# Copies and casts of a fused attention and gated-convolution kernel moved from ACT to DVE and POOL, with a new order table

## The chip, the core and the metric

The kernel runs on one core of one Trainium2 chip. The metric is the device time of one execution in microseconds (us), lower is better; three executions of the kernel before are given. Besides the times there is one profiled execution with its trace. The engines are PE (matmul; PEld is its weight load), DVE, ACT, POOL, and SP, which here only issues DMAs.

## What is computed

The reference, cut to what matters (B = 4, H = 8 heads, S = 768, D = 64, so d_model = 512):

```python
k_sum = k.reshape(B, H, 24, 32, D).max(axis=3)
v_sum = v.reshape(B, H, 24, 32, D).mean(axis=3)
scores = concat([where(|i - j| < 16, q @ k.T / 8, -1e9), q @ k_sum.T / 8 + log(32)])
a = softmax(scores)
x = (a @ concat([v, v_sum])).transpose(0, 2, 1, 3).reshape(B, S, 512)
gate = sigmoid(sum over 5 taps k of conv_w[k] * x shifted by 4 - k)
out = (gate * (x @ w_val)) @ w_out
```

## The kernel before, in words

The work is cut into 24 units u (batch, third of the sequence, half of the heads; six units to a batch) and 12 groups g = u // 2 of 256 rows. Each step of a unit or group is a small function `op_X`, and the table `ORDER` (L51) lists about 1,130 tokens such as `S.7.0` (step S of unit 7, part 0). The program is emitted token by token in this order, so the table sets the order of every engine's queue and of SP's DMA issues; an engine takes its own tokens in turn and waits at the first that isn't ready. All instructions of one engine stay in the table's order, whatever the others do.

The steps, with lines and engines as they are before:

- Loads by SP: `k` (484 KB), `q` (512 KB), `v` (512 KB), `n` (values, 256 or 384 KB), `w` and `o` (the two weight matrices, four parts each of 512 KB), `m`, `i`, `c`; `f` copies a block of rows of `v` in the buffer.
- `ks` (L307, L310, DVE) block maxima of k, `kc` (L315, POOL) copies them into the k tile. `S` (L438, PE, 16 matmuls) scores, `N` (L454, DVE, 4 instructions) mask and row minimum, `E` (L468, ACT, 4 instructions) exponential, `R` (DVE) reciprocal, `M` (L481, POOL) scaling.
- `T` (L490, PE, 16 transposes) into PSUM, `C` (L494, ACT) copies it out, `X` (L508, PE, 32 matmuls) attention times values.
- The result x of a unit is read out of PSUM by `F` (L519, ACT, as f32), `H` (L516, ACT, rounded), and `I` (L533, ACT, times the last tap, into the PSUM tile g, one of two halves). `A` (L538, DVE, eight per unit) adds the other taps, `G` (L544, ACT) is the tanh of the gate, `L` (L524, POOL) the rest of x after rounding.
- `V` (L558, PE) is x times w_val: 24 matmuls, 16 in group 0; `gf` (L563, DVE) gates it; `gh` (L567, ACT) rounds it and `gl` (L572, POOL) takes the rest; `O` (L587, PE, 12 matmuls, 8 in group 0) is the last product; `oe` (L597, ACT) brings it out of PSUM and `st` (L606, SP) stores it. `oe` writes a tile `ob` with two buffers, so the third needs the store of an earlier one to have landed.
- The weights are split on chip: `wvs`/`wos` (ACT), `wvd`, `wve`, `wod`, `woe` (DVE), then the rounded part `wvc`/`woc` (`high_part`, ACT or, with a trailing 1, POOL), then `wvb`/`wob` (POOL). `pw` are eight blocks of matmuls on a constant, early in the program.

PSUM is given out by `psum_plan` from the same table: scores S and transposes T share a ring of two pairs of banks, everything else a ring of four. A PE step whose place in the ring is still held by an earlier tile waits until that tile's last reader is through.

Of the kernel before, what the change touches and what calls it, by code (L numbers as in the profile page):

```python
# [56 lines left out]
wve.1 ce T.0 E.3.2 q.2 S.4.0 S.4.1 N.4.3 N.4.0 n.0.5 pw.5 E.1.1 E.1.3 E.1.0 VB.5 pw.7 VB.3 R.1 R.3
N.4.1 w.2 M.1.1 C.0.0 C.0.1 wvc.1 wvd.2 w.3 wvs.3 wvd.3 N.4.2 v.0.0 M.1.0 wvs.2 wve.2 wve.3 VB.1
vb.0 pw.2 wvb.1 h.0 S.5.0 S.5.1 N.5.2 N.5.0 wvc.3.1 M.3.1 M.3.0 N.5.3 v.0.1 N.5.1 vb.1 T.1 C.1.0
k.1.0 ks.1.0 wvb.3 wvc.2.1 C.1.1 X.0 I.0.0 F.0 I.0.1 A.0.0 A.0.1 X.1 F.1 I.1.0 A.1.0 T.2 n.1.3 v.1.1  # L60
o.0 E.5.0 v.1.0 tr.1.3.1 wvb.0 A.0.2 A.0.3 I.1.1 V.0.0 E.5.1 E.4.1 k.1.1 A.1.1 n.1.1 E.4.3 C.2.0
E.4.2 kc.1.0 A.0.4 A.1.2 A.0.5 A.1.3 A.0.6 E.5.3 A.1.4 A.0.7 G.0 A.1.5 C.2.1 q.3 ks.1.1 kc.1.1 wvb.2
# [636 lines left out]
```

## Time and profile before

| | us |
|---|---|
| three executions | 234.11, 232.50, 232.01 |
| median | 232.5 |
| profiled execution, its own time | 233.51 |
| its span in the trace (first to last instruction) | 231.4 |
| PE busy / DVE / ACT / POOL in the span | 218.8 / 171.0 / 187.1 / 150.9 |

The span is what the trace can explain; the remaining 2.1 us of the profiled execution lie around it. The granted PE clock is full speed in every slice. PE is busy 95% of the span, but a busy PE is not a PE at its best, since the time of a matmul in the trace includes waits inside a block; so the argument counts blocks of PE work by their price when they follow each other closely.

### The profile page before, as it was taken

Reading aid. Unit: us, or ns where it says so; the run is one execution under the profiler, and the core shown is the slowest. Engines: PE = TensorE matmul, PEld = TensorE weight load, DVE = VectorE, ACT = ScalarE, POOL = GpSimd, SP = SyncE. Lnnn points to the kernel's source line nnn. Section 1 sums busy time; section 2 is a strip of 40 time slices with the busy share of each in tenths; the row PEclk is TensorE's granted clock in tenths of the full one; section 3 lists DMA queues with packets and bytes.
Section 4 is the critical chain, followed back from the end, with each engine's and each line's share of the span. In section 5 each row is a group of like instructions: output and inputs, shape, how many; then the busy total and the mean of one; then the engine's idle time right before and its main releaser. Section 6 shows DMA issues by size and latency. Waiting matters only on the chain.

```text
span 231.4 us, 7645 instructions
## 1 busy us (share of the span) xinstructions
PE 218.8 (95%) x2828; PEld 185.3 (80%) x2828; DVE 171.0 (74%) x699; ACT 187.1 (81%) x614; POOL 150.9 (65%) x207
## 2 busy tenths in 40 slices
PE   2699999989999989999999999999999999999993
PEld 2475687638998867999789899988989898899882
DVE  1698989989999988869998859639729848555600
ACT  2399899999999979998999987798996698553320
POOL 2125897987999999956497869699069419044040
PEclk9999999999999999999999999999999999999999
DMA  6999999995986946828915634540449310102122
GB/s 235 341 389 369 408 410 281 406 364 179 318 353 217 283 174 219 305 82 290 284 29 184 183 118 140 180 177 3 130 145 319 89 48 19 46 0 93 45 91 91
DMA packets 17052, 46.50 MB, mean 201 GB/s; under 512 B 2136, under 2 KB 3160, under 8 KB 17016
## 3 DMA queue, kind: packets, MB, share of 16 engines
q1 hardware_dynamic: 17016, 46.02, 57.1%
q8 instruction: 22, 0.36, 0.6%
q14 instruction: 14, 0.11, 0.2%
HBM read 37.56 MB, written 6.29 MB: 190 GB/s over the span
## 4 chain that ended last, share of the span: by engine, by line
PE 66%; DMA 18%; ACT 10%; DVE 4%; issue 1%; SPq 1%; ACTq 0%
PE out L587 23%; PE val L558 23%; DMA k<-in_kT_dram 7%; PE s L438 7%; PE x L508 7%; DMA raw_wo<-in_wo_dram 5%; ACT p L468 4%; PE pt L490 4%; DMA out_dram<-ob 3%; DMA qbd<-in_qT_dram 3%; DVE g L538 2%; PE pw L332 1%; PE vb L342 1%; ACT g L533 1%; DVE sn L454 1%
## 5 line engine op out<-in xcount | busy, mean ns | idle before, releaser
L538 DVE SCALAR_TENSOR_TENSOR g<-xf,cwt,g 128x256 f32<-128x256 f32 x192 | 87.5, 484 | 14.3 <-ACT g L533 8.6
L468 ACT ACTIVATE p<-sn,nm 128x120 f32<-128x120 f32 x192 | 74.0, 396 | 10.5 <-DVE nm L454 10.3
L481 POOL TENSOR_TENSOR p<-p,ri 128x480 f32<-128x480 f32 x48 | 46.8, 991 | 23.9 <-DVE ri L476 21.5
L558 PE MATMUL val<-xh,wv 128*128 128x256 f32 x352 | 49.6, 283 | 0.0
L454 DVE CUSTOM_DVE_ANT_0 sn<-s,mask 128x120 f32<-128x120 f32 x192 | 42.7, 276 | 6.0 <-PE s L438 4.5
L558 PEld LDWEIGHTS val<-xh,wv 128*128 128x128 f32 x352 | 44.5, 188 | 1.4 <-issue 0.3
L587 PE MATMUL out<-wo,gh 128*128 128x512 f32 x176 | 45.1, 398 | 0.0
L572 POOL TENSOR_TENSOR gl<-gf,gh 128x512 fp32r<-128x512 f32 x22 | 28.3, 1294 | 18.1 <-ACT gh L567 18.0
L468 ACT ACTIVATION_READ_ACCUMULATOR p<-sn,nm 128x1 f32 x192 | 38.3, 200 | 0.0
L587 PEld LDWEIGHTS out<-wo,gh 128*128 128x128 f32 x176 | 31.7, 188 | 6.9 <-ACT gt L544 0.2
L524 POOL TENSOR_TENSOR xl<-xf,xh 128x512 fp32r<-128x512 f32 x22 | 28.2, 1292 | 7.9 <-ACT xh L516 7.8
L438 PE MATMUL s<-k,qbd 64*64 64x120 f32 x768 | 26.3, 280 | 6.9 <-POOL k L315 2.7
L438 PEld LDWEIGHTS s<-k,qbd 64*64 64x64 f32 x768 | 21.0, 139 | 11.1 <-POOL k L315 3.9
L326 POOL TENSOR_TENSOR vT<-vT 128x384 f32<-128x384 f32 (+3 forms) x48 | 27.3, 570 | 2.8
L597 ACT ACTIVATE ob<-out 128x512 f32<-128x512 f32 x23 | 13.7, 597 | 18.1 <-PE out L587 14.5
L558 PE MATMUL val<-xl,wv 128*128 128x256 f32 x176 | 27.7, 279 | 0.0
L494 ACT COPY pts<-pt 120x512 f32<-120x512 f32 x48 | 26.3, 589 | 1.5 <-PE pt L490 1.4
L508 PEld LDWEIGHTS x<-pts,v 120*64 120x64 f32 x768 | 23.6, 138 | 3.7 <-ACT pts L494 1.1
L508 PE MATMUL x<-pts,v 120*64 120x64 f32 x768 | 25.4, 224 | 0.4 <-DVE low_wo L394 0.4
L563 DVE SCALAR_TENSOR_TENSOR gf<-gt,val 128x512 f32<-128x512 f32 x24 | 16.4, 685 | 11.9 <-PE val L558 5.7
L587 PE MATMUL out<-wo,gl 128*128 128x512 f32 x88 | 24.1, 395 | 0.0
L558 PEld LDWEIGHTS val<-xl,wv 128*128 128x128 f32 x176 | 23.7, 188 | 0.0
(55 smaller groups left out, 259.1 us busy)
## 6 DMA issues: line engine op xcount, KB each, us to landing
v<-in_vw_dram SPq DMA_DIRECT2D x24, 512.0 KB
k<-in_kT_dram SPq DMA_DIRECT2D x16, 484.0 KB
out_dram<-ob SPq DMA_DIRECT2D x23, 256.0 KB
qbd<-in_qT_dram SPq DMA_DIRECT2D x11, 512.0 KB
vT<-in_vT_dram SPq DMA_DIRECT2D x12, 384.0 KB
raw_wv<-in_wv_dram SPq DMA_DIRECT2D x4, 512.0 KB
raw_wo<-in_wo_dram SPq DMA_DIRECT2D x4, 512.0 KB
v<-vs SPq DMA_DIRECT2D x18, 96.0 KB
```

The costliest lines, as they stand in the source:

```text
L326: nc.gpsimd.tensor_tensor(dst, src[:, :, :n], src[:, :, n : 2 * n], ALU.add)
L438: nc.tensor.matmul(sp[64 * e : 64 * e + 64, h, c * KW : c * KW + KW], qbd[g % NQB][64 * h : 64 * h + 64, pr, i * QT : i * QT + QT], ktile( ...
L454: nc.vector.tensor_tensor_reduce(sn[:, n, :], tiles["s", u][:, h, c * KW : c * KW + KW], mask[:, mv, :], -1.0 / math.sqrt(D), 3.0e38, ALU.add,
L468: nc.scalar.activation(p[:, n, :], tiles["sn", u][:, n, :], AF.Exp, bias=tiles["nm", u][:, n : n + 1], scale=-1.0, accum_out=rs[:, u % NRS ...
L481: nc.gpsimd.tensor_tensor(p[:, w], p[:, w], ri[:, w].unsqueeze(2).broadcast_to([P, TPU, KW]), ALU.mult)
L494: nc.scalar.copy(pts[:, :, QT * e : QT * e + QT], tiles["pt", u][:KW, e])
L508: nc.tensor.matmul(dst, w, src, start=True, stop=True)
L524: nc.gpsimd.tensor_tensor(xl[:, prs(u), :], xf(g)[:, prs(u), HALO:], tiles["xh", g][:, prs(u), :].bitcast(F32), ALU.subtract,)
L538: nc.vector.scalar_tensor_tensor(gt, xf(u // NHP)[:, pr, o : o + SG], cwt[:, pr, o : o + 1], gt, ALU.mult, ALU.add)
L558: nc.tensor.matmul(val[:, r], w, x, start=(n == 0), stop=(n == len(terms) - 1))
L572: nc.gpsimd.tensor_tensor(gl[:, cos, :], tiles["gf", g, cp], tiles["gh", g][:, cos, :].bitcast(F32), ALU.subtract)
L587: nc.tensor.matmul(po, x, w, start=(n == 0), stop=(n == len(terms) - 1))
```

## The change

Six steps get an optional last argument `alt`; a token that carries it as a trailing 1 runs on another engine:

- `C`, `H`, `F`, `I`, `oe` (copies out of PSUM): DVE rather than ACT, by a new helper `copy` (tensor_copy, or tensor_scalar with a factor).
- `gh` (cast of the gated values, SBUF to SBUF): POOL rather than ACT.
- `wvc`/`woc` could do so before; three more now do (all eight on POOL).

The same steps are all there: none is added or removed. Of the tokens that change engine, 11 are `C`, 11 `I`, 8 `H`, 3 `F`, 3 `oe` (36 copies to DVE), 15 `gh` and 3 weight casts (18 to POOL). `vb` gets the argument too, but no token uses it. The order table is new from the first token to the last, and with it the queues, the order of the loads and the places in PSUM. The diff, cut:

```diff
-    def op_C(u, e):
+    def copy(dst, src, scale=None, alt=0):
+        if alt and scale is None:
+            nc.vector.tensor_copy(dst, src)
+        elif alt:
+            nc.vector.tensor_scalar(dst, src, scale, None, ALU.mult)
+        elif scale is None:
+            nc.scalar.copy(dst, src)
+        else:
+            nc.scalar.activation(dst, src, AF.Copy, scale=scale)
+
+    def op_C(u, e, alt=0):
         pts = wt(("pts", u), [KW, NP, P], "pts")
-        nc.scalar.copy(pts[:, :, QT * e : QT * e + QT], tiles["pt", u][:KW, e])
+        copy(pts[:, :, QT * e : QT * e + QT], tiles["pt", u][:KW, e], alt=alt)
...
-        nc.scalar.activation(gt[:, r], src, AF.Copy, scale=cwt[:, pr, NK - 1 : NK])
+        copy(gt[:, r], src, cwt[:, pr, NK - 1 : NK], alt)
...
-        nc.scalar.copy(gh[:, 2 * cp : 2 * cp + 2, :], tiles["gf", g, cp])
+        (nc.gpsimd.tensor_copy if alt else nc.scalar.copy)(
+            gh[:, 2 * cp : 2 * cp + 2, :], tiles["gf", g, cp]
+        )
...
-            nc.scalar.activation(ob, po, AF.Copy, scale=0.5)
+            copy(ob, po, 0.5, alt)
```

Some lines of the new table that the text below speaks of: the loads and DVE work ahead of `S.7.0`, the stretch after it, and one of the late stores.

```diff
+woe.1 F.2 E.5.1 o.2 wos.2 v.2.1 H.2 E.5.3 L.3 L.2 h.2 wod.2 woe.2 O.0.1 O.0.0 N.6.2 E.6.2 N.6.3 R.5
+N.8.1 N.8.2 M.5.1 I.2.0 N.6.0 I.3.0 k.1.2 N.6.1 ks.1.2 oe.0.1 E.6.3 I.3.1 E.6.0 k.1.3 v.2.0 M.5.0
+ks.1.3 n.1.3 A.3.0 N.8.3 N.8.0 I.2.1 kc.1.2 woc.2.1 kc.1.3 T.4 A.2.0 A.3.1 E.6.1 R.6 st.0.1 tr.1.3.1
+A.2.1 A.3.2 S.7.0 E.8.1 C.4.0 f.2.0 C.4.1 oe.0.0 S.7.1 N.7.3 E.7.3 f.2.1 X.4 n.1.1 tr.1.1 woc.0.1
...
+E.17.2 C.14.0.1 oe.4.0 A.12.6 h.7 O.4.1 v.7.1 gf.6.1 C.15.1.1 R.17 f.7.1 k.3.1 ks.3.1 A.12.7 C.14.1
+kc.3.3 n.3.2 v.8.1 C.15.0 tr.3.1 X.15 I.15.1.1 st.4.0 E.16.2 oe.4.1 E.16.3 st.4.1 I.15.0 H.15.1 F.15
...
+X.16 H.16.1 I.16.0 X.17 v.9.1 st.3.1 F.16 F.17 I.16.1 S.20.1 S.21.0 S.20.0 h.9 gh.7.1.1 L.16 N.20.0
```

## Rows read from the trace of the kernel before

**Rows 1.** The page, part 1: busy time, share of the span, instructions
```profile
PE 218.8 (95%) x2828; PEld 185.3 (80%) x2828; DVE 171.0 (74%) x699; ACT 187.1 (81%) x614; POOL 150.9 (65%) x207
```

**Rows 2.** Stages: length, busy of PE, PEld, DVE, ACT, POOL; PEclk, DMA, GB/s
```profile
40.00:50.00 10.00, 9.72 (x126) 5.89 (x126) 8.88 (x36) 10.00 (x33) 9.42 (x14) 1.00 1.03 407
50.00:60.00 10.00, 9.37 (x174) 7.70 (x173) 9.89 (x51) 9.87 (x42) 8.28 (x13) 1.00 0.67 221
60.00:70.00 10.00, 10.00 (x122) 9.60 (x121) 9.72 (x44) 9.95 (x32) 9.43 (x12) 1.00 0.92 337
70.00:80.00 10.00, 10.00 (x144) 7.97 (x144) 9.42 (x36) 9.97 (x35) 9.65 (x15) 1.00 0.85 262
80.00:87.00 7.00, 5.73 (x92) 4.50 (x91) 6.17 (x14) 5.50 (x17) 6.69 (x13) 1.00 0.50 173
...
120.00:140.00 20.00, 20.00 (x273) 18.18 (x269) 15.75 (x73) 18.29 (x62) 15.23 (x23) 1.00 0.45 142
```

**Rows 3.** PE in order of time: start, us, line, operation, idle before and releaser
```profile
51.85 0.64 PE L438 MATMUL s<-k,qbd 64*64 64x120 f32 x16 [0.63 <-DVE nm L454]
...
87.05 1.46 PE L438 MATMUL s<-k,qbd 64*64 64x120 f32 x48 [1.32 <-ACT pts L494]
```

**Rows 4.** The chain that ended last: start, us until the next piece, what
```profile
39.64 8.94 DMA k<-in_kT_dram
...
49.62 0.79 DVE g L538 x2
...
52.00 0.65 DVE ks L307
52.65 0.26 DVE ks L310
...
57.71 2.27 ACT p L468 x12
...
63.44 1.04 ACT gh L567 x2
64.48 0.75 ACT g L533 x2
...
69.29 0.47 ACT pts L494
...
77.90 7.94 DMA out_dram<-ob
...
99.05 0.44 PE vsp L358 x4
...
102.12 1.80 PE s L438 x64
...
112.50 1.09 PE pt L490 x32
113.59 2.97 PE out L587 x12
...
118.36 2.02 PE x L508 x64
120.38 8.68 PE val L558 x72
...
213.90 13.87 PE out L587 x60
```

**Rows 5.** DVE in order of time, two 512-wide instructions back to back
```profile
43.94 0.68 DVE L563 SCALAR_TENSOR_TENSOR gf<-gt,val 128x512 f32<-128x512 f32 x1
44.54 0.68 DVE L402 SCALAR_TENSOR_TENSOR wf<-sc_wo,low_wo 128x512 uint32<-128x512 uint32 x1
```

**Rows 6.** Groups by line: busy us, mean ns of one; a cast on POOL
```profile
L409 POOL CAST wo<-wf 128x512 fp32r<-128x512 f32 x2 | 1.2, 612 | 0.1
```

**Rows 7.** The casts' partner gl (L572) on POOL in two stages: length, busy
```profile
60.00:80.00 20.00, 3.90 (x3) 1.00 0.88 299
200.00:231.40 31.40, 5.09 (x4) 1.00 0.16 59
```

More of the change, by code (lines that the diff above doesn't have):

```diff
@@ L57 @@
[L57 to L62, printed above, removed]
@@ new lines @@
+N.12.3 gl.2.1 O.2.1 oe.2.1 X.8 R.11 gf.3.0 V.3.1 N.13.3 N.12.1 A.9.2 N.13.2 H.8 F.8 N.12.2 A.9.3
+I.8.1 v.5.1 N.13.1 A.9.4 I.8.0 A.9.5 A.8.0 E.12.3 E.12.1 tr.2.0 n.2.3 st.2.1 f.5.1 q.8 f.5.0 M.10.0
+T.10 C.10.0 M.11.1 M.11.0 T.11 C.11.1 C.11.0 A.8.1 gf.3.1 A.9.6 A.8.2 A.9.7 E.13.1 E.12.2 A.8.3
+A.8.4 G.9 C.10.1 O.2.0 oe.2.0 X.11 tr.2.2 A.8.5 E.13.2 R.12 A.8.6 A.8.7 X.10 S.15.1 S.14.1 S.14.0
+F.10 S.15.0 I.10.0 G.8 L.8 tr.2.3 ks.3.0 n.3.0 h.5 I.10.1.1 H.10.1 N.15.2 VS.2 E.13.3 R.13 A.10.0
+N.14.0 gh.3.0.1 L.9 F.11 V.4.0 vs.2 N.15.3 I.11.0 h.6 M.12.1 H.11 E.15.2 I.11.1.1 gl.3.0 N.14.1
@@ new lines @@
+N.15.1 A.11.0 M.13.1 N.14.2 A.11.1 gf.4.0 E.15.1 E.14.0 V.4.1 A.10.1 E.14.1 E.15.3 L.10 gh.4.0
+gh.3.1.1 gl.3.1 M.12.0 O.3.0 N.14.3 A.10.2 A.10.3 E.14.3 A.11.2 A.10.4 N.15.0 gf.4.1 T.12 A.11.3
+A.11.4 A.11.5 E.14.2 A.11.6 st.2.0 M.13.0 T.13 C.13.0 C.12.1 A.11.7 E.15.0 oe.3.0 C.13.1.1 R.15
+C.12.0 G.11 O.3.1 oe.3.1 L.11 v.6.0 f.6.0 v.6.1 f.6.1 X.13 A.10.5 F.13 X.12 H.13 I.13.1 kc.3.0
+gl.4.0 tr.3.0 v.7.0 k.3.3 ks.3.2 S.16.1 S.16.0 S.17.0 q.9 A.10.6 S.17.1 n.3.1 f.7.0 ks.3.3 A.10.7
+I.13.0 G.10 V.5.0 kc.3.2 gh.4.1.1 gl.4.1 I.12.1 M.15.0 F.12 N.16.1 I.12.0 N.17.1 H.12.1 L.12 L.13
@@ new lines @@
+S.23.1 S.23.0 N.23.2 E.23.2 N.23.3 E.23.3 N.23.1 E.23.1 N.22.2 N.22.3 N.23.0 E.23.0 O.7.0 oe.7.0
+A.18.2 A.18.3 L.19 M.21.0 L.18 V.9.1 A.19.1 A.18.4 E.22.3 E.22.0 A.19.2 M.20.1 R.23 M.23.0 gl.8.1
+M.23.1 N.22.1 A.18.5 gl.8.0 E.22.1 A.18.6 A.19.3 A.18.7 G.18 A.19.4 A.19.5 E.22.2 V.9.0 T.20 T.21
+C.21.0 A.19.6 R.22 M.22.1 C.20.0 C.20.1 C.21.1.1 v.10.1 f.10.0 f.11.1 gf.9.0 A.19.7 G.19 gf.9.1
+O.7.1 st.7.0 f.10.1 X.20 oe.7.1 I.20.0 X.21 I.21.1 M.22.0 h.10 st.7.1 gh.9.1.1 T.22 C.22.1 H.21
+F.20.1 T.23 I.20.1.1 H.20.1 L.20 O.8.0 I.21.0.1 gl.9.1 F.21.1 L.21 gh.9.0 gl.9.0 A.21.0 A.20.0
@@ L124 @@
+st.10.1 O.11.0 oe.11.0.1 st.11.0 O.11.1 oe.11.1 st.11.1
 """
@@ L348, in op_VB, with op_vb @@
         )
-    def op_vb(e):
+    def op_vb(e, alt=0):
         rows = slice(BOFF[e], BOFF[e] + NB)
         src = tiles["vb", 0][rows].unsqueeze(1).broadcast_to([NB, VP, DM])
-        nc.scalar.activation(vtile(0)[rows, e], src, AF.Copy, scale=1.0 / BLK)
+        copy(vtile(0)[rows, e], src, 1.0 / BLK, alt)
     def op_VS(b):
@@ L511, in prs, with op_H, op_F @@
         return slice(2 * (u % NHP), 2 * (u % NHP) + 2)
-    def op_H(u):
+    def op_H(u, alt=0):
         g = u // NHP
         xh = wt(("xh", g), [P, NPR, SG], "xh", F32R)
-        nc.scalar.copy(xh[:, prs(u), :], tiles["x", u])
-    def op_F(u):
-        nc.scalar.copy(xf(u // NHP)[:, prs(u), HALO:], tiles["x", u])
+        copy(xh[:, prs(u), :], tiles["x", u], alt=alt)
+    def op_F(u, alt=0):
+        copy(xf(u // NHP)[:, prs(u), HALO:], tiles["x", u], alt=alt)
     def op_L(u):
@@ L527, in op_L, with op_I @@
         )
-    def op_I(u, r):
+    def op_I(u, r, alt=0):
         gt = ps(("g", u), [P, 2, SG])
```

117 lines of the change are left out of this document (49 added, 68 removed).

## The prediction

> **What bounds the kernel now.** First the page's busy times [rows 1]: PE 218.8 of 231.4 us, then ACT with 187.1, DVE 171.0, POOL 150.9. PE is nearest to the span, so the question is where PE stands idle or runs thin, and what it waits for there. Then the stages [rows 2]: from 50 to 80 us DVE and ACT are busy 94 to 100% and POOL 83 to 97%, so PE shares this stretch with three engines that are as full as it is; from 120 to 140 us PE has 20.00 of 20.00, ACT 18.29 and the others have room. Then the chain of waits in order of time [rows 4]: up to 48.6 us it ends in loads (the last a k tile, 39.64 to 48.58), then runs through DVE and, from about 56 to 78 us, through ACT (exponentials, copies, casts in one closed row), then a store; from 87.05 us to 227.76 it is PE alone. Last, PE's own timeline [rows 3]: S.7.0 starts at 51.85 after a wait for DVE (N of unit 8), S.12.1 at 87.05 after 1.32 us for ACT's copy C. From 87.05 us on PE has no gap, so nothing that only lightens ACT there gives a microsecond. What the change can win lies ahead of 87 us.
>
> How much is that? I count PE's work between the two rows of [rows 3] at its price when blocks follow each other closely [rows 4]: S 1.80/4 = 0.45, T 1.09/2 = 0.55, X 2.02/2 = 1.01, V 8.68/3 = 2.89, O between 13.87/5 = 2.77 and 2.97, so 2.87, VS 0.44. From S.7.0 to just before S.12.1 the old table has 9 S, 5 T, 5 X, 4 V, 3 O and one VS: 4.05 + 2.75 + 5.05 + 11.56 + 8.61 + 0.44 = 32.5 us. It took 87.05 - 51.85 = 35.2 us, so 2.7 us are lost. The share that one row names is 1.32 us; the rest is thin blocks. The trace agrees that ACT is the cause: ACT is full there [rows 2].
>
> A second measure gives more. The Trainium skill (Perfetto Trace Analysis, Identifying the Most-Contended Engine) says that busy matmuls are a poor measure of PE's headroom and that busy weight loads are a better one. By the rows, weight loads are busy 18.18 of 20 us = 0.91 where PE is closed, but 7.70 + 9.60 + 7.97 + 4.50 = 29.8 of 37 us from 50 to 87 us [rows 2]; at 0.91 that is 32.7 us of work, so 4.3 us would be lost, not 2.7. By that measure the sum below would end 1.6 us lower. I keep the count of blocks, since the loads' share also moves with the mix of blocks, and take the other as a rival.
>
> **The change part by part.** *Off ACT.* 25 copies of full width at 0.47 (C, H, F, oe), 11 I at 0.75/2 = 0.375, 15 gh and 3 weight casts at 1.04/2 = 0.52 [rows 4]: 11.8 + 4.1 + 9.4 = 25.3 us, so ACT falls to 162. Most is after 87 us, where PE is closed, and worth nothing by itself. What counts is ACT's queue ahead of an early PE step. For X.11, at 101 us before, ACT must be through C of unit 11. Ahead of that the new table has 4 E fewer (0.757 each by 2.27/3: 3.0), 2 C (0.9), 2 I (0.75), one oe and one vs (0.9), 3 gh and 3 weight casts (3.1): 8.7 us less. PE's own list ahead of X.11 is shorter by one X and one VS, 1.5 us. So ACT is 7.2 us earlier against PE, of which 4.3 come from moved work (a C, two I, the gh and the casts) and the rest from the order. That is more than the 2.7 us lost, so ACT stops holding PE between 52 and 87 us. I leave 0.2 for hand-overs: gain 2.5.
>
> *Onto DVE.* No row shows DVE copying scores or x out of PSUM. The nearest are two 512-wide instructions with an operand in PSUM, which follow each other in 0.60 us [rows 5]; bounds are ACT's 0.47 and the same with its whole length, 0.68. I take 0.60; for the half-width I the step of A, 0.79/2 = 0.395 [rows 4], between 0.30 and 0.60. Sum 25 x 0.60 + 11 x 0.395 = 19.3 us (15.1 to 23.6): DVE goes to 190, under PE's 219. Only C.0.1, I.4.0 and I.9.0 lie ahead of V.3.0, so the full stretch gets 1.4 us of it. By that point the new order has DVE no later against PE: ahead of O.1.1 its list is 1.2 us longer and PE's 1.0. After 100 us DVE's remaining list is about 83 us beside 115 of PE: it lies beside matmuls. Were that cover gone, each copy would cost its 0.60.
>
> *Onto POOL.* 18 casts at 0.61 [rows 6], 11 us: POOL 162 of 231. A cast now stands in POOL's queue ahead of its own gl, so 0.61 on a path that was ACT's 0.52: nothing. After 100 us POOL's list is about 74 us beside 115 of PE. At the end of the program V.11.1 is followed by three O (8.3 us) before O.11.0 needs its operands; two gf (1.2), two casts (1.2) and two gl (1.3 each [rows 7]) are 5.0 us: hidden, with 3.3 to spare. The tail behind the last O is unchanged.
>
> *The gate at 52 us.* S.7.0 has the same PE work ahead of it in both tables. It needs a load, a ks and a kc, and N of unit 8. The loads ahead of k.1.2 add up to 15.4 MB instead of 15.7: 0.3 MB at 407 GB/s [rows 2] is 0.7 us earlier. DVE's list ahead of the needed N is longer by one ks (0.91) and one C (0.60) and shorter by two A (0.79) [rows 4]: 0.7 us later. So 0. Bounds: 1.0 us earlier if loads alone decide; 1.2 us later, two waits like the 0.63 at S.7.0 [rows 3], since O.0.1 needs the weight part loaded last (now o.2, the third of four) one step earlier, and since f.2.0 and f.2.1, behind a store, are wanted by X.4 soon after.
>
> *Order of PE's blocks, and the first 15 us.* 89 changes between kinds of block instead of 94, at 0.1 to 0.2 each by the two prices of O: 0.2 to my count. The head waits on the same tiles in another order: 0.
>
> Sum: 231.4 - 2.5 - 0.2 = 228.7 for the span. The profiled execution took 233.51, 2.1 more than its span and 1.0 above the median of 232.5; I take the difference from the median: 232.5 - 2.7 = **229.8 us**.
>
> **The rivals.** *The gate moves (0.2).* The loads, not ACT, set the time to 52 us, and the new table asks for X.4 earlier behind S.7.0. If PE gets away from S.7.0 and X.4 2.7 us later than before, the gain is gone: 231.5 to 234. For it: the chain ends in loads until 48.6, DMA share 1.03. Against it: as many bytes ahead.
>
> *More than counted (0.12).* If weight loads tell the truth, 4.3 - 0.2 + 0.2 = 4.3 us go: 228.2, and with the gate 1.0 earlier 227.2.
>
> *One output buffer: slower (0.14).* The new table leaves st.3.1 until after oe.5.0, and st.5.0 until after oe.8.0. As `ob` has two buffers, for most of the stretch from O.4.0 to O.8.0 only one is left, and each oe waits for the store before it to land. A store took 7.94 us in a busy stretch [rows 4]. O.4.0 and O.4.1 end 2 x 0.55 + 2.87 = 4.0 us apart; with 0.5 for the copy, oe.4.1 comes up to 4.5 us late, and ACT's whole queue behind it (E of unit 16) waits too. By the table ACT has about 13 us of lead on PE there, so PE stands only if a PSUM bank is missed. It decides from landings of about 4 us: two of the three close pairs (4, 6, 8) at 2 to 3 us, on a kernel that otherwise gains 0 to 2.7, give 233 to 236.
>
> *Shared port (0.04).* POOL's casts could be held up by a fuller DVE. Three gl took 3.90 us where DVE is 94 to 97% busy [rows 2, 7] and four took 5.09 at the end of the program: 1.30 and 1.27. If each cast cost one DVE copy more, POOL would have 11 us more, hidden but for the few ahead of close O: 230.5 to 232. The Trainium skill (Perfetto Trace Analysis, Optimizing Scalar/DVE Operations) warns that the two share an SBUF read port, so that moving work between them may not help; the trace doesn't show that here.
>
> That the change doesn't do what it says is excluded: each engine is written out in the table.
>
> **How the numbers follow.** The forecast (ACT's lead frees 52 to 87 us) gets 0.45, by itself 228.5 to 231.2; the rivals 0.2, 0.12, 0.14, 0.04, and 0.05 for a stall I don't see, 233 and more. A measurement of this kernel tells about 1% (2.3 us) from no change. Faster by that, below 230.2: 0.33 of the forecast, 0.12 and 0.02 of the port: 0.47. Slower, above 234.8: 0.07 of the buffer, 0.03 of the gate, 0.04 unseen: 0.14. Same: 0.39. For 8 in 10 the range runs from 227.6 to 233.4.
>
> **What would show it.** Right: S.7.0 again near 52 us, no PE wait for ACT between 52 and 87 us, the block that stood at 87.05 reached near 84.5 for equal work, PE closed from there, ACT near 162 and DVE near 190. Wrong: S.7.0 or X.4 later than 53 (gate); ACT waits for out_dram followed by PE gaps around O.4.1 (buffer); DVE's copies at 0.8 or more; PE gaps after 100 us released by DVE.

## The result, and the profile after

The changed kernel takes 234.93 us (median; the kernel before, beside it, 232.50): ratio 1.0104, 95% interval 1.0083 to 1.0124. The forecast was 229.8 us, so faster; the kernel is 1% slower. The profiled execution took 234.08 us with a span of 232.0, so it lies 0.9 under its median, as the profiled one of before lay 1.0 above its own. The two traces differ by 0.6 us where the medians differ by 2.4, so one more trace of each kernel was taken (below).

The busy times of the page are those that the prediction worked out (ACT 162, DVE 190, POOL 162) [rows 1]:

```profile
PE 218.7 (94%) x2828; PEld 184.7 (80%) x2828; DVE 188.6 (81%) x735; ACT 162.6 (70%) x560; POOL 161.2 (69%) x225
```

The stages, with the columns of [rows 2] (length; busy of PE, PEld, DVE, ACT, POOL; PEclk, DMA share, GB/s):

```profile
70.00:80.00 10.00, 10.00 (x146) 7.92 (x143) 9.55 (x37) 9.39 (x26) 9.46 (x18) 1.00 0.69 235
80.00:87.00 7.00, 7.00 (x120) 6.46 (x116) 6.04 (x19) 6.34 (x25) 6.84 (x8) 1.00 0.86 308
120.00:140.00 20.00, 19.76 (x249) 17.20 (x249) 16.91 (x58) 11.97 (x42) 14.18 (x22) 1.00 0.42 145
138.00:149.00 11.00, 10.59 (x71) 9.21 (x69) 10.82 (x51) 5.05 (x22) 10.19 (x12) 1.00 0.71 232
180.00:200.00 20.00, 19.61 (x235) 17.86 (x234) 17.16 (x43) 10.69 (x32) 12.35 (x13) 1.00 0.13 46
```

From 80 to 87 us PE is closed where it was 5.73 of 7 before [rows 2]. But from 120 us on, where the chain of before was PE alone [rows 4], it isn't: 19.76 of 20, 10.59 of 11, 19.61 of 20. ACT is half empty there, and DVE is full from 138 to 149 us. The waits of PE between 100 and 232 us in the changed kernel (waiting engine, line, what ended the wait: us in total, times, longest); in the kernel before PE had none there:

```profile
PE out L600 <- ACT g L501: 1.1, 2, 0.8
PE val L569 <- POOL xl L535: 0.4, 1, 0.4
PE out L600 <- DVE xh L495: 0.4, 1, 0.4
PE val L569 <- DVE g L497: 0.3, 1, 0.3
PE out L600 <- ACT gt L555: 0.2, 1, 0.2
```

**One measure for all runs.** For each PE block I take its start less the prices of all PE blocks ahead of it in its own table (the prediction's prices; V and O of group 0 at 3.55 and 3.75, VB 0.93, `pw` 0.5 and the long one 2.0, read from the same traces). The result is the time that PE has lost by then; only differences between kernels mean something. X.0 (28 us) has the same blocks ahead of it in both tables, X.15 stands near 133 us, and the last O ends the program.

| kernel | ratio to before (95%) | lost by X.0 | by X.15 | by the last O | behind X.15 |
|---|---|---|---|---|---|
| before, first trace | | 10.4 | 15.5 | 14.9 | -0.6 |
| before, second trace (e10) | | 10.8 | 13.6 | 13.1 | -0.5 |
| after, first trace | 1.0104 (1.0083 to 1.0124) | 8.2 | 12.3 | 15.4 | 3.1 |
| after, second trace (e11) | | 8.1 | 13.0 | 16.1 | 3.1 |
| e1 readers of x on ACT | 1.0259 (1.0211 to 1.0307) | 8.3 | 13.5 | 20.5 | 6.9 |
| e2 one engine for each late x | 1.0019 (0.9989 to 1.0050) | 8.1 | 14.4 | 16.0 | 1.6 |
| e3 new order, old engines | 1.0885 (1.0814 to 1.0956) | 8.2 | 18.3 | 33.9 | 15.6 |
| e4 old order, new engines | 1.0725 (1.0676 to 1.0773) | 11.8 | 24.6 | 31.1 | 6.5 |
| e5 new up to X.15, then old | 1.0010 (0.9976 to 1.0045) | 8.3 | 12.7 | 13.5 | 0.8 |
| e6 old up to X.15, then new | 1.0135 (1.0091 to 1.0179) | 10.7 | 14.9 | 17.8 | 2.9 |
| e7 new up to X.16, then old | 1.0131 (1.0069 to 1.0193) | 8.2 | 11.9 | 15.7 | 3.8 |
| e8 after, three stores earlier | 1.0638 (1.0590 to 1.0687) | 8.1 | 26.0 | 29.1 | 3.0 |
| e9 after, two PE blocks moved | 1.0273 (1.0232 to 1.0315) | 8.1 | 12.3 | 17.9 | 5.7 |
| e12 new head, then old | 0.9969 (0.9944 to 0.9993) | 8.5 | 13.1 | 12.8 | -0.3 |
| e13 old head, then new | 1.0166 (1.0133 to 1.0199) | 11.3 | 14.6 | 17.5 | 2.9 |
| e14 as e5, late copies moved | 1.0268 (1.0235 to 1.0301) | 9.0 | 12.9 | 20.3 | 7.4 |
| e15 after, late copies not moved | 1.0630 (1.0592 to 1.0668) | 8.6 | 13.3 | 28.9 | 15.6 |
| e16 after, four copies back | 1.0178 (1.0138 to 1.0217) | 8.6 | 14.3 | 18.6 | 4.3 |
| e17 e9 with four copies back | 1.0295 (1.0262 to 1.0328) | 8.3 | 13.7 | 21.5 | 7.8 |
| e18 after, three copies back | 1.0041 (1.0014 to 1.0067) | 8.3 | 13.6 | 15.8 | 2.2 |

The two traces of each kernel already tell the story: by X.15 the changed kernel is ahead by 1.9 us on the mean of two (14.6 less 12.7; e6, which runs the old table up to there, has 14.9), and behind X.15 it loses 3.1 us each time where the kernel before gains 0.5. Together 1.7 us slower; the medians say 2.4, with 1.9 to 2.9 by the interval.

The chain of waits of the changed kernel ahead of O.7.0 shows what such a late loss is made of (start us, us until the next piece, what):

```profile
172.80 0.49 DVE g L497
173.30 0.60 DVE xh L495
...
173.97 0.59 ACT xf L499
174.56 0.72 ACT g L501 x2
...
175.33 2.83 PE out L600 x11
```

These are the four readers of x.18 (I, H, F, I), two on each engine, one after the other. O.7.0 takes over the PSUM place of x.18 and starts when the last is through. Between X.18 and O.7.0 PE has four S, 1.8 us; four readers take 2.5.

### The profile page after: what moved, and what is told of

The parts are those of the page before. It is cut to its first block, busy times and chain, and to the rows that moved or that the text cites. A ratio compares the mean times of both kernels' runs of the same rounds, so it can differ in the third digit from the quotient of the medians.

```text
span 232.0 us, 7667 instructions
## 1 busy us (share of the span) xinstructions
PE 218.7 (94%) x2828; PEld 184.7 (80%) x2828; DVE 188.6 (81%) x735; ACT 162.6 (70%) x560; POOL 161.2 (69%) x225
## 4 chain that ended last, share of the span: by engine, by line
PE 63%; ACT 17%; DVE 10%; POOL 5%; issue 2%; DMA 2%; SPq 0%; ACTq 0%; DVEq 0%
PE out L600 25%; PE val L569 19%; PE x L519 6%; ACT p L469 6%; PE s L439 6%; PE pt L491 3%; DVE g L549 3%; PE vb L343 3%; ACT g L501 2%; ACT xf L499 2%; DVE sn L455 2%; ACT pts L499 2%; DMA k<-in_kT_dram 2%; POOL p L482 2%; DVE g L497 1%
## 5 line engine op out<-in xcount | busy, mean ns | idle before, releaser
L600 PE MATMUL out<-wo,gh 128*128 128x512 f32 x176 | 45.8, 402 | 1.7 <-ACT g L501 1.1
L535 POOL TENSOR_TENSOR xl<-xf,xh 128x512 fp32r<-128x512 f32 x22 | 28.2, 1289 | 12.7 <-DVE xh L495 8.9
L469 ACT ACTIVATION_READ_ACCUMULATOR p<-sn,nm 128x1 f32 x192 | 37.0, 193 | 0.0
L439 PE MATMUL s<-k,qbd 64*64 64x120 f32 x768 | 25.3, 279 | 4.0 <-POOL k L316 3.8
L585 POOL TENSOR_TENSOR gl<-gf,gh 128x512 fp32r<-128x512 f32 x22 | 28.4, 1296 | 0.8 <-PE out L600 0.4
L519 PE MATMUL x<-pts,v 120*64 120x64 f32 x768 | 26.2, 224 | 1.0 <-ACT gt L555 0.7
L555 ACT ACTIVATE gt<-g 128x512 f32<-128x512 f32 x24 | 14.1, 599 | 15.7 <-DVE g L549 15.7
L499 ACT COPY pts<-pt 120x512 f32<-120x512 f32 x37 | 20.6, 587 | 4.1 <-DVE pts L495 2.2
L578 POOL CAST gh<-gf 128x512 fp32r<-128x512 f32 x15 | 9.1, 613 | 17.9 <-DVE gf L574 12.5
```

The costliest lines, as they stand in the source:

```text
L439: nc.tensor.matmul(sp[64 * e : 64 * e + 64, h, c * KW : c * KW + KW], qbd[g % NQB][64 * h : 64 * h + 64, pr, i * QT : i * QT + QT], ktile( ...
L469: nc.scalar.activation(p[:, n, :], tiles["sn", u][:, n, :], AF.Exp, bias=tiles["nm", u][:, n : n + 1], scale=-1.0, accum_out=rs[:, u % NRS ...
L499: nc.scalar.copy(dst, src)
L519: nc.tensor.matmul(dst, w, src, start=True, stop=True)
L535: nc.gpsimd.tensor_tensor(xl[:, prs(u), :], xf(g)[:, prs(u), HALO:], tiles["xh", g][:, prs(u), :].bitcast(F32), ALU.subtract,)
L585: nc.gpsimd.tensor_tensor(gl[:, cos, :], tiles["gf", g, cp], tiles["gh", g][:, cos, :].bitcast(F32), ALU.subtract)
```

## The experiments

Three theories went into the first four runs: the hand-over of one x tile between ACT and DVE costs; DVE is too full late; or late stores leave one output buffer. From e5 on each expectation names its own cases.

### e1 to e4: engines and order taken apart

e1: the 22 copies and scalings of x (11 I, 8 H, 3 F) that had gone to DVE are back on ACT, in the new order.

```diff
-kc.3.3 n.3.2 v.8.1 C.15.0 tr.3.1 X.15 I.15.1.1 st.4.0 E.16.2 oe.4.1 E.16.3 st.4.1 I.15.0 H.15.1 F.15
+kc.3.3 n.3.2 v.8.1 C.15.0 tr.3.1 X.15 I.15.1 st.4.0 E.16.2 oe.4.1 E.16.3 st.4.1 I.15.0 H.15 F.15
...
```

> The changed kernel with its order table kept, but all 22 copies and scalings that read x (11 I, 8 H, 3 F) back on ACT; 11 C, 3 oe and the 15 gh and 3 weight casts stay moved. Theory 1 (hand-over: two engines that read one PSUM tile do so one after the other in the order of the table, so a tile split between ACT and DVE makes each wait in turn for the other's queue): the PE waits after 130 us go, about 3 us, ratio to the kernel before 0.985 to 0.995. Theory 2 (DVE is too full in the last 100 us): DVE loses 22 copies, about 11 us, so it improves too, ratio 0.985 to 1.0. Theory 3 (late stores leave one output buffer): nothing changes, ratio 1.01.

Measured 1.0259: all three theories missed. The largest waits of PE behind 60 us:

```profile
PE out L599 <- ACT xh L498: 2.0, 1, 2.0
PE x L518 <- ACT ob L500: 1.8, 1, 1.8
```

DVE was 10 us emptier (178.2), ACT 171.4 of 237 us, and still PE lost 6.9 us behind X.15. So neither the hand-over nor a full DVE is the whole of it; both of these waits end at ACT.

e2: DVE keeps 17 late readers of x, but whole tiles: x.15, 17, 18 and 20 go to DVE, those of the other units from 12 on to ACT (H.12 stays on DVE). DVE's busy time is the same, 188.7 us.

```diff
-G.12 A.15.0 X.14 I.14.1.1 F.14 H.14.1 S.19.1 kc.3.1 S.18.1 gl.5.1 A.15.1 A.15.2 R.16 S.18.0 L.14
+F.15.1 G.12 A.15.0 X.14 I.14.1 F.14 H.14 S.19.1 kc.3.1 S.18.1 gl.5.1 A.15.1 A.15.2 R.16 S.18.0 L.14
...
```

> The changed kernel with its order table kept and as many x readers on DVE after unit 12 as it has (17), but not split within a tile: units 15, 17, 18 and 20 read by DVE alone, H of unit 12 stays on DVE, the rest of units 12 to 23 on ACT. DVE's load is that of the changed kernel within 0.3 us. Theory 1 (hand-over): the late PE waits go or fall below 1 us, ratio to the kernel before 0.985 to 0.998. Theory 2 (DVE too full): no change, ratio 1.008 to 1.012. Theory 3 (one output buffer): no change, ratio 1.01.

Measured 1.0019, between the cases of its theories: the same load on DVE, laid out otherwise, is worth 0.85%. A full DVE as such is not the cause. But the wait at O.7.0 stayed, though all four readers of x.18 were now on DVE, so that a split tile is not what makes it:

```profile
PE out L600 <- DVE g L497: 0.9, 1, 0.9
```

e3 has the new table with the 54 tokens on their old engines, e4 the old table with the 54 on their new engines.

> The new order table with every copy and cast on the engine that it had before: the order alone. Theory 1 (hand-over): no tile is split, so no late waits; the early gain of the new order stays but for the 4.3 us that ACT has more to do ahead of 87 us, ratio 0.985 to 1.0. Theory 2 (DVE too full): the same, ratio 0.985 to 1.0. Theory 3 (one output buffer, an effect of the order): the loss stays, ratio 1.01 or more.

> The old order table with the 54 copies and casts on their new engines: the moves alone. Theory 1 (hand-over): tiles of units 14 to 18 and 20 to 23 are split here too, late PE waits of 2 to 4 us appear that the kernel before does not have, ratio 1.0 to 1.02, with part of the wait at 87 us gone. Theory 2 (DVE too full): the same late loss. Theory 3 (late stores): no late loss, since the stores of the old order are early, ratio 0.985 to 1.0.

Measured 1.0885 for e3 and 1.0725 for e4. Theories 1 and 2 missed both, and theory 3, which for e3 said only "1.01 or more", missed e4. The two halves of the change cost 7 to 9% each and together 1%. In e3 ACT is busy 186.9 us of 250.5, 75%, less than the 81% before: no engine is full, and PE loses 20 us more than before. Order and placement are one fit; neither has a price of its own.

### e5 to e8: where the loss lies, and the stores

At X.15 the two tables have done nearly the same work (11 tokens differ), so they can be joined there; the joint is called the seam. e5 runs the new table up to there and the old one behind it, on the old engines; e6 the reverse; e7 is e5 with the seam at X.16.

```diff
-C.14.1 kc.3.3 n.3.2 v.8.1 C.15.0 tr.3.1 X.15 I.15.1.1 st.4.0 E.16.2 oe.4.1 E.16.3
+C.14.1 kc.3.3 n.3.2 v.8.1 C.15.0 st.3.1 v.8.0 f.8.0 E.16.3 E.16.2 G.12 oe.4.1 st.4.1
...
```

> The first 753 tokens are those of the new table with their new engines (up to the one ahead of X.15, 132.75 us in the changed kernel's trace), all the rest follow in the old table's order on their old engines (the two tables have done nearly the same work there: 11 tokens differ). Theory A, the gain and the loss lie in two separate stretches: at the seam the changed kernel has lost about 12.4 us of PE's time against 15 us in the kernel before, and the old rest loses nothing more, so 232.5 - 2.6 = about 229.9 us, ratio 0.985 to 0.993. Theory B, the order and the engines are one fit over the whole span and any seam breaks it, as in the two runs with order alone (1.0885) and moves alone (1.0725): 1.02 or more. Theory C, late stores: the three stores put off lie partly in this half (st.3.1), little difference to A.

> The mirror of the run before: the first 754 tokens of the old table on their old engines (up to the one ahead of X.15), the rest in the new table's order on the new engines. Theory A: the 15 us lost by 133 us as in the kernel before, and then the 3 us more that the changed kernel loses after 133 us: 235 to 236.5 us, ratio 1.011 to 1.017, above the changed kernel's 1.0104. Theory B (one fit, a seam breaks it): 1.02 or more. Rival to A, the loss late comes only because PE is ahead early and the other engines then catch up with it: no loss late here, ratio 0.997 to 1.003.

> As the first of these runs, with the seam at 848 tokens (ahead of X.16, 153.5 us in the changed kernel's trace; 10 tokens differ there). Theory A: the changed kernel has by then lost 13.7 us, 1.3 more than at X.15, so about 231.2 us, ratio 0.991 to 0.998, between the first run and the changed kernel. Theory B: 1.02 or more.

e6, 1.0135, is as its theory A had it, and its loss behind X.15 (2.9 us) is the changed kernel's (3.1). So the late loss belongs to the late half, whatever went before. e5 missed its 0.985 to 0.993: by its trace it has the early lead and loses 0.8 us at the seam, but its median is that of the kernel before. Its span of 230.0 us lies 1.4 under that of the first trace of before while the medians don't differ, which made that first trace suspect (e10). By the medians the early lead comes to 0.3%, 0.7 us (e6 against the changed kernel), and those two intervals overlap. e7 missed too: at X.16, V.7.0 has been pulled out from in front of it, and X.16 waits for copies C (1.8 us lost there, 0.8 at X.17).

e8: the changed kernel with the late stores right behind their `oe`.

```diff
-C.12.0 G.11 O.3.1 oe.3.1 L.11 v.6.0 f.6.0 v.6.1 f.6.1 X.13 A.10.5 F.13 X.12 H.13 I.13.1 kc.3.0
+C.12.0 G.11 O.3.1 oe.3.1 st.3.1 L.11 v.6.0 f.6.0 v.6.1 f.6.1 X.13 A.10.5 F.13 X.12 H.13 I.13.1
...
```

> The changed kernel with its three late stores moved: st.3.1, st.5.0 and st.8.0 stand right behind their oe.3.1, oe.5.0 and oe.8.0 in the table, and nothing else differs. Theory A (the loss is in the readers of PSUM, not in the stores): as the changed kernel, 1.007 to 1.014. Theory C (an output buffer is missing while a store stands late): the late loss goes, 0.99 to 1.002.

Measured 1.0638, outside both cases, and for a reason neither had: SP is a queue too. The trace of e8, SP's issues and PE's matmuls in order of time (start, us, engine, line, operation, idle before and releaser):

```profile
98.63 17.11 SPq L619 DMA_DIRECT2D out_dram<-ob  x2
115.83 0.38 SPq L286 DMA_DIRECT2D v<-in_vw_dram  x1
119.22 0.82 SPq L369 DMA_DIRECT2D v<-vs  x1
```

```profile
121.94 1.12 PE L519 MATMUL x<-pts,v 120*64 120x64 f32 x16 [7.39 <-DMA v<-vs]
126.12 2.83 PE L519 MATMUL x<-pts,v 120*64 120x64 f32 x48 [3.06 <-DMA v<-vs]
```

The two stores form one row of 17 us: the second waited for oe.3.1, the load of v behind it waited with it, and X.13 stood 7.4 us ahead of its first 16 matmuls and 3.1 us ahead of its other 16 (the x48 are these and the 32 of X.12). Putting a store "late" behind the loads is what the new order needs. As to the question asked: the losses at O.7.0 and O.8.0 are there unchanged, 3.0 us behind X.15 although the stores are early. The rival of the output buffer is out.

### e10, e11: a second trace of each kernel

> The kernel before itself, for a second trace. Its first trace is of an execution 1.0 us above its median. Theory A (the 2.7 us lost between S.7.0 and S.12.1 belong to the kernel): they are there again, within 0.5 us. Theory B (a good part of them belongs to that one execution): less than 1.7 us are lost there in this one, and the whole is near 232.5 us.

> The changed kernel itself, for a second trace. Its first trace is of an execution 0.85 us below its median. Theory A (the loss behind 130 us belongs to the kernel: 0.84 us at O.5.0, 0.50 at O.6.1, 0.83 at O.7.0, 0.51 at O.8.0, 0.38 at V.11.0): the same five again, within 0.4 us each, and what is more than in the first trace lies earlier, in waits for transfers. Theory B (the late waits are those of one execution): at most three of the five are there.

e11 (234.56 us) gives the same late losses, as its theory A had it: 3.1 us behind X.15, the same five waits of PE. e10 (231.65 us) gives another early half, as its theory B had it. From S.7.0 to S.12.1 the first trace of before lost 2.7 us, the second 1.4; the changed kernel lost 1.7 in both of its traces. The difference is one thing, seen on ACT (columns as above). First trace of the kernel before:

```profile
82.88 1.55 ACT L494 COPY pts<-pt 120x512 f32<-120x512 f32 x3
85.93 0.60 ACT L597 ACTIVATE ob<-out 128x512 f32<-128x512 f32 x1 [1.50 <-DMA out_dram<-ob]
86.42 0.58 ACT L494 COPY pts<-pt 120x512 f32<-120x512 f32 x1
```

Second trace of the kernel before, ACT and then PE:

```profile
82.55 1.56 ACT L494 COPY pts<-pt 120x512 f32<-120x512 f32 x3
84.03 0.60 ACT L597 ACTIVATE ob<-out 128x512 f32<-128x512 f32 x1
84.53 0.58 ACT L494 COPY pts<-pt 120x512 f32<-120x512 f32 x1
```

```profile
84.80 1.87 PE L438 MATMUL s<-k,qbd 64*64 64x120 f32 x64
```

In the first execution an `oe` stood 1.50 us for a store to free its buffer, the copy C.9.0 stood behind it, and S.12.1, which takes the PSUM place that C.9.0 reads, stood 1.32 [rows 3]. In the second the store had landed, and the four S follow without a gap. The row that the prediction read as "ACT is full" was ACT idle behind one late store; from 80 to 87 us ACT is busy only 5.50 of 7 us [rows 2].

This is not peculiar to that one execution. e6 runs the same table on the same engines up to X.15, and in its trace the wait is there again (ACT):

```profile
85.45 0.60 ACT L501 ACTIVATE ob<-out 128x512 f32<-128x512 f32 x1 [1.36 <-DMA out_dram<-ob]
```

S.12.1 stands 1.17 us behind it, and 2.8 us are lost from S.7.0 to S.12.1. In e12 (below), which has the old order there too, the store is in time and 1.2 us are lost. So the wait comes in two of four traces of that order; how often it comes in the executions that were only timed is not known.

### e12, e13: the head

> Only the head of the new table: its first 143 tokens (to about 29 us, where the two tables differ by 6 tokens; loads in the new order, one copy C and three casts of weights on their new engines), all the rest in the old order on the old engines. Theory A (the early gain is the head's: in two traces of the kernel before X.0 stands 10.4 and 10.8 us behind its close-packed place, in two of the changed kernel 8.1 and 8.2): about 1.2 us of it last to the end, 231.0 to 231.8 us, ratio 0.993 to 0.998. Theory B (the gain of the early half comes from ACT's lighter load between 30 and 97 us): 0.999 to 1.003, the head's gain being lost again at the loads that S.7.0 waits for.

> The mirror: the first 147 tokens of the old table on their old engines, the rest in the new order on the new engines. Theory A: the changed kernel without the head's gain, so 1.2 us longer, 235.7 to 236.7 us, ratio 1.014 to 1.019. Theory B: as the changed kernel, 1.008 to 1.013.

e12 takes only the new table's first 143 tokens (to 29 us):

```diff
-mset pw.4 pw.6 k.0.1 ks.0.1 kc.0.1 q.1 k.0.0 q0.1 ks.0.0 kc.0.0 S.2.1 m N.2.3 E.2.3 N.2.2 E.2.2 S.0.1
+k.0.0 mset pw.5 pw.7 ks.0.0 kc.0.0 k.0.1 ks.0.1 q0.1 kc.0.1 S.0.1 c q0.0 S.0.0 m q.1 cd S.2.0 S.2.1
...
```

Measured 0.9969 and 1.0166, both as theory A: the lead at X.0 is made in the head. e3, with every copy and cast on its old engine, has the new table's 8.2 us at X.0 too, so the order gives it, and not the two tokens of the head that change engine (C.0.1 and wvc.1). PE's first blocks in the second trace of the kernel before, and in e12:

```profile
5.57 1.08 PE L438 MATMUL s<-k,qbd 64*64 64x120 f32 x16 [2.24 <-POOL k L315]
8.59 1.08 PE L438 MATMUL s<-k,qbd 64*64 64x120 f32 x16 [1.94 <-DMA qbd<-in_qT_dram]
10.17 2.05 PE L438 MATMUL s<-k,qbd 64*64 64x120 f32 x32 [0.50 <-issue]
```

```profile
6.74 1.88 PE L438 MATMUL s<-k,qbd 64*64 64x120 f32 x32 [3.42 <-POOL k L315]
8.92 1.75 PE L438 MATMUL s<-k,qbd 64*64 64x120 f32 x32 [0.30 <-DMA qbd<-in_qT_dram]
10.59 2.35 PE L332 MATMUL pw<-ones 128*64 128x104 f32 x24
```

The old table asks second for the whole `q.1` (512 KB) and starts with an S that needs it; the new one asks for two k tiles and a 128 KB part of q, starts later, and then has two S at a time. X.0 starts at 26.09 us in e12 against 28.34. Not all of the 2 us lasts: S.7.0 starts at 51.04 against 51.85 and 51.36, 0.3 to 0.8 earlier; what takes the rest back in between was not traced. With the old head ahead of the new order (e13) S.7.0 starts at 52.43, against 49.75 and 50.1 in the changed kernel. With 0.31% (0.07 to 0.56) e12 is the one kernel here that beats both.

### e14, e15: engines and order apart, in the late half only

35 of the 54 moved tokens lie behind X.15. e14 is e5 with those 35 on their new engines; e15 is the changed kernel with those 35 on their old engines.

```diff
-I.15.0 I.15.1 F.15 H.15 kc.3.1 S.19.0 N.19.0 F.14 h.8 gl.5.1 I.14.0 S.18.0 I.14.1 S.18.1 N.18.2 R.16
+I.15.0 I.15.1.1 F.15 H.15.1 kc.3.1 S.19.0 N.19.0 F.14 h.8 gl.5.1 I.14.0 S.18.0 I.14.1.1 S.18.1
...
```

> As the run with the new table up to the token ahead of X.15 and the old order behind it (ratio 1.001), but the 35 moved copies and casts that lie behind the seam go to their new engines. Tells whether the late loss lies in the engines or in the order. Theory A (the order of TensorE's blocks sets it, and in the old order a V or another O stands between an x block and the O that takes its place): the loss at O.7.0 and O.8.0 stays away, 1.000 to 1.006. Theory B (the engines set it, since DVE is full between 138 and 149 us and the old order was laid out for copies on ACT): 1.01 to 1.04, with TensorE waiting for DVE.

> The new table throughout, but the 35 moved copies and casts behind the token ahead of X.15 stay on their old engines. Theory A (the order of the blocks sets the late loss): the waits at O.7.0 and O.8.0 are there and no smaller than in the changed kernel (0.8 and 0.5 us), ratio 1.01 or more. Theory B (the new engines set it): less than the changed kernel's 1.0104.

With the first half the same in all four, the late half reads: old order and old engines 1.001, old order and new engines 1.027, new order and old engines 1.063, both new 1.010. So the moves cost 2.6% in an order laid out for ACT, and the new order gives most, not all, of it back; it would itself cost 6% with the copies on ACT. e14 came out as theory B, e15 as theory A: the causes don't divide into engine or order. One wait of each, PE in order of time, e14 first:

```profile
145.12 1.21 PE L569 MATMUL val<-xh,wv 128*128 128x256 f32 x8 [1.55 <-DVE gf L574]
```

```profile
182.01 1.20 PE L599 MATMUL out<-wo,gh 128*128 128x512 f32 x4 [2.39 <-ACT g L500]
```

In e14, V.7.1 takes the place of val 6,0 and waits for gf.6.0, which DVE reaches at 144.39 though V.6.0 ended at 140.77: ahead of it DVE does an H, seven A and N. In e15, O.7.0 waits for the same four readers of x.18 as in the changed kernel, now all behind an ACT that has reached them 2 us later.

### e9, e16, e17, e18: single places in the late half

In the old order a V (2.9 us) stands between the four S behind an X pair and the O that takes over the place of x.17 (O.6.1) or of x.18 (O.7.1); here the four S and V.8.1 in the first trace of the kernel before:

```profile
171.29 1.87 PE L438 MATMUL s<-k,qbd 64*64 64x120 f32 x64
173.09 1.21 PE L558 MATMUL val<-xh,wv 128*128 128x256 f32 x8
```

The V was needed: in the same trace the last reader of x.17 (H.17, on ACT) ends only 0.6 us before the O.6.1 that takes its place, less than the 2.9 us of the V ahead of it.

```profile
157.83 0.61 ACT L516 CAST xh<-x 128x512 fp32r<-128x512 f32 x1
```

```profile
159.07 2.01 PE L587 MATMUL out<-wo,gh 128*128 128x512 f32 x8
```

In the new order O.6.1 (in the place of x.16) and O.7.0 (x.18) stand right behind the four S, O.8.0 (x.20) behind X.21 and two T, and V.11.0 (x.23) behind one O. Each starts as the last reader ends: O.6.1 at 157.71 (157.65), O.7.0 at 175.33 (175.28), O.8.0 at 191.58 (191.43), V.11.0 at 208.37 (208.32). The distance alone doesn't decide. In the old order O.4.0 has four S and one X between x.15 and itself, as O.6.1 now has behind x.16, and doesn't wait: ACT reads x.15 in one row of 1.9 us (134.32 to 136.24), while the readers of x.16 take 2.6 us on two engines, the last of them behind F.17 in ACT's queue. e9 gives O.6.1 a V ahead of it again:

```diff
-N.18.2 O.5.0 oe.5.0 T.17 T.16
+N.18.2 T.17 T.16
...
-R.19 M.19.0 VS.3 vs.3 G.14 E.18.2 C.17.0.1 C.17.1.1 E.18.1 V.7.0 gf.7.0 gh.7.0
+R.19 M.19.0 VS.3 O.5.0 oe.5.0 vs.3 G.14 E.18.2 C.17.0.1 C.17.1.1 E.18.1
...
-S.21.1 I.17.0 f.9.0 I.17.1 f.9.1 A.17.0 A.16.1 N.21.1 A.16.2 v.11.1
+S.21.1 V.7.0 I.17.0 f.9.0 I.17.1 f.9.1 A.17.0 A.16.1 N.21.1 A.16.2 gf.7.0 gh.7.0 v.11.1
```

> The changed kernel with two blocks of TensorE moved, every instruction on the engine that the changed kernel gives it: O.5.0 (with its oe) from ahead of T.17 to behind VS.3, and V.7.0 (with its gf and gh) from ahead of X.16 to behind S.21.1. In the changed kernel O.5.0 waits 0.84 us for gf.6.0 (place of val 6,0), and O.6.1 0.50 us for the four readers of x.16, which hold the place that it takes; in the kernel before a V stands between the S blocks and that O. Theory A (the late loss is the distance on TensorE between a place's last matmul and the block that takes the place over): both losses go, at most 0.4 us come back at X.17, which needs C.17.1: 233.5 to 234.1 us, ratio 1.003 to 1.008. Theory B (the other engines are too full late, the wait only moves on to the next block): 1.009 to 1.014, with losses at X.16, X.17 or V.7.0 as large as those removed.

The loss at O.6.1 went, 0.50 to 0.1 us, as A had it, and the kernel is 1.7% slower than the changed one, as B had it and worse. The largest wait, in PE's order of time:

```profile
148.07 1.16 PE L491 MATMUL pt<-ident,p 64*120 64x64 f32 x32 [1.88 <-DVE nm L455]
```

T.17 now comes 2.9 us sooner and takes the place of the scores of unit 19, which N.19.1 on DVE reads until 147.9, at the end of the stretch in which DVE is full. VS.3 behind it waits 0.8 us more, for POOL (vsT, the block sums of v). One statement in this expectation, in that of e11 and in that of e16 was wrong: O.5.0 doesn't wait for gf.6.0, which is through at 144.67. Of the 0.84 us counted there 0.3 lie at O.5.1, which waits for the tanh of unit 12 on ACT, and 0.5 inside V.7.1 just ahead, which waits for the low part of x.15 from POOL:

```profile
144.33 0.51 PE L569 MATMUL val<-xl,wv 128*128 128x256 f32 x2 [0.41 <-POOL xl L535]
```

The chain of the changed kernel ahead of that (pieces in order of time):

```profile
136.91 0.41 DVE g L497
...
137.34 0.60 ACT xf L499
...
137.96 0.70 DVE xh L495
...
138.73 1.29 POOL xl L535
140.03 2.84 POOL p L482 x3
...
143.03 1.24 POOL xl L535
```

The readers of x.14 change engine twice, and POOL's queue of L, three M and L follows from the last of them. e16 therefore puts I.15.1, H.15, I.14.1 and H.14 back on ACT, half empty here.

```diff
-kc.3.3 n.3.2 v.8.1 C.15.0 tr.3.1 X.15 I.15.1.1 st.4.0 E.16.2 oe.4.1 E.16.3 st.4.1 I.15.0 H.15.1 F.15
-G.12 A.15.0 X.14 I.14.1.1 F.14 H.14.1 S.19.1 kc.3.1 S.18.1 gl.5.1 A.15.1 A.15.2 R.16 S.18.0 L.14
+kc.3.3 n.3.2 v.8.1 C.15.0 tr.3.1 X.15 I.15.1 st.4.0 E.16.2 oe.4.1 E.16.3 st.4.1 I.15.0 H.15 F.15
+G.12 A.15.0 X.14 I.14.1 F.14 H.14 S.19.1 kc.3.1 S.18.1 gl.5.1 A.15.1 A.15.2 R.16 S.18.0 L.14
```

> The changed kernel with four copies back on ACT: I.15.1, H.15, I.14.1 and H.14, 2.3 us off DVE just ahead of 138 to 149 us, where DVE is busy 10.82 of 11 us and ACT 5.05 (a half, so there is room). Theory A (that local fullness of DVE makes gf.6.0 late, for which O.5.0 waits 0.84 us): the loss at O.5.0 goes or halves, the later ones stay: 1.005 to 1.009. Theory B (no room is to be had so: the same copies wait in ACT's queue, as when all 22 were put back, ratio 1.0259): 1.010 or more.

> The run with the two blocks swapped (O.5.0 behind VS.3, V.7.0 behind S.21.1; ratio 1.0273), and the same four copies back on ACT. There T.17 waited 1.88 us for N.19.1 on DVE. Theory A (DVE's local fullness): N.19.1 comes about 2 us earlier, T.17's wait goes for the most part, 1.014 to 1.021. Theory B (the swap costs by something else): 1.023 to 1.032.

Measured 1.0178 for e16, as theory B, yet both cases hold at their own place. The loss at O.5.1 and V.7.1 is gone (16.2 us lost at X.14, 16.2 at O.5.0), but 1.9 us are lost at X.14. ACT and then PE in e16:

```profile
133.66 0.59 ACT L499 COPY pts<-pt 120x512 f32<-120x512 f32 x1 [0.88 <-DVE pts L495]
135.92 0.45 ACT L501 ACTIVATE g<-x,cwt 128x256 f32<-128x256 f32 x1 [1.67 <-PE x L519]
...
137.05 0.58 ACT L501 ACTIVATE ob<-out 128x512 f32<-128x512 f32 x1
```

```profile
137.68 1.15 PE L519 MATMUL x<-pts,v 120*64 120x64 f32 x32 [1.81 <-ACT ob L501]
```

I.15.1 is the first thing to read x.15. On ACT it waits 1.67 us for X.15, with E.16.2 and oe.4.1 behind it in the queue; X.14 takes the place that oe.4.1 reads, and stands 1.81. e1 has the same wait of 1.8 at the same block. e17 (1.0295, its theory B) has it too, and its wait at T.17 fell only from 1.88 to 1.5.

So e18: as e16, with I.15.1 left on DVE. One instruction differs.

```diff
-kc.3.3 n.3.2 v.8.1 C.15.0 tr.3.1 X.15 I.15.1 st.4.0 E.16.2 oe.4.1 E.16.3 st.4.1 I.15.0 H.15 F.15
+kc.3.3 n.3.2 v.8.1 C.15.0 tr.3.1 X.15 I.15.1.1 st.4.0 E.16.2 oe.4.1 E.16.3 st.4.1 I.15.0 H.15 F.15
```

> As the run that put I.15.1, H.15, I.14.1 and H.14 back on ACT (ratio 1.0178), but I.15.1 stays on DVE: one instruction differs. In that run ACT waited at I.15.1 for X.15 with E.16.2 and oe.4.1 behind it in its queue, and X.14, which takes the place of out 4,1, waited 1.81 us for oe.4.1; the loss at O.5.0 was gone (16.22 us at X.14, 16.16 at O.5.0). Theory A (what counts is what stands behind a copy that waits, not how full the engine is): the wait at X.14 goes with this one instruction, the loss at O.5.0 stays away, 1.003 to 1.009. Theory B (the other three cost on ACT as well): 1.010 to 1.018.

Measured 1.0041 (1.0014 to 1.0067), as theory A. One half-width copy of 0.45 us on ACT or on DVE is worth 1.4% of the kernel. ACT in e18 at the same place, and PE's two X, now in one row:

```profile
134.22 0.58 ACT L501 ACTIVATE ob<-out 128x512 f32<-128x512 f32 x1
```

```profile
134.02 2.08 PE L519 MATMUL x<-pts,v 120*64 120x64 f32 x64
```

e18 is also better than the changed kernel, by 0.6%: the intervals don't meet. The three copies it put back (H.15, I.14.1, H.14, 1.9 us on DVE) are part of the late loss; with them gone it is 2.2 us instead of 3.1, and what remains is O.6.1, O.7.0, O.8.0 and V.11.0, the places of x.

## Why the prediction was wrong, point by point

- **The early term, 2.5 us off ACT between S.7.0 and S.12.1: failed.** The step "the trace agrees that ACT is the cause: ACT is full there" took a wait named ACT for an ACT without time; its own rows have ACT busy 5.50 of 7 us around that wait. 1.3 of the 2.7 us were one store that lands late in some executions (before and e6, not e10 and e12); of the rest nothing was won: 1.4 us are lost there in the second trace of before, 1.7 in both of after. So a lighter ACT was worth 1.0 to 1.1 us where the store came late and nothing where it didn't. The second measure, by weight loads, was further off (4.3 us).
- **"The head waits on the same tiles in another order: 0": failed.** The order of the first loads and S is worth 2 us at X.0 (e3, e12) and the head 0.3 to 0.6% at the end (e12, and e13 against the changed kernel). The gate at S.7.0, put at 0 within -1.0 and +1.2, came at 49.75 and 50.1 us instead of 51.85 and 51.36: 1.3 to 2.1 earlier, of which the head alone gives 0.3 to 0.8; the new order without its head comes later than before (52.43, e13).
- **"After 100 us DVE's remaining list is about 83 us beside 115 of PE: it lies beside matmuls", price 0: failed, and decided the sign.** PE loses 3.1 us behind X.15 where it had lost nothing. The sum over a stretch couldn't see it. It isn't the busy time that PE waits for but single instructions: the last reader of a PSUM place that the next O takes over, and what stands behind a waiting copy in an in-order queue. Of PE's closed rows after 87 us the prediction concluded that nothing could be won; it should have asked how close the next thing stood (0.6 us at O.6.1), and the new table moved it closer.
- **Prices and busy times: right.** DVE's copies out of PSUM take steps of 0.60, the half-width I a step of 0.40 where a reader follows on DVE (172.80 to 173.20, its whole length 0.49; 0.395 was taken), the cast on POOL 613 ns. ACT 162.6, DVE 188.6, POOL 161.2. Every one of these was right, and the time was wrong. One small term doesn't follow from its own figures: five changes of block fewer at 0.1 to 0.2 are 0.5 to 1.0, not 0.2; no run shows it by itself.
- **The rivals.** The gate moved, but forwards. One output buffer: in the changed kernel no copy waits for a store, and with early stores the late loss is the same (e8); right was that SP's place of a store matters, in the other direction. Shared port: the 22 `gl` take 1296 ns on the mean with a fuller DVE, 1.27 to 1.30 before [rows 7]: nothing. What came is the case "a stall I don't see", given 0.05. Its time was named among the signs of failure ("PE gaps after 100 us released by DVE"), but not priced, and by the five waits only 0.7 of 2.4 us end at DVE; 1.3 end at ACT and 0.4 at POOL.
- **The change doesn't divide.** The prediction summed parts: off ACT, onto DVE, order. Order alone is +8.9%, moves alone +7.3%, both +1.0%. No sum of parts gives that.

Open: why the new order puts an O right behind four S, where e9 shows that a V there makes T.17 wait for DVE, is a question to the table as a whole; whether another order with these engines beats e12 was not tried. Which of the head's edits (the loads' order or S's) carries the 2 us was not separated. That the readers of x set the losses at O.6.1, O.7.0, O.8.0 and V.11.0 is read from the traces: no run takes these four away in the new order, and in e9, which takes one, others came.
